# Linear attention and feed-forward on one core: k side of a batch first, k shifted by its maxima in PSUM, and a job order read from a table

## The chip, the cores and the metric

The kernel runs on one core of a Trainium2 chip. The metric is device microseconds of one execution. Each comparison below is made in rounds on one chip, in which the kernel under test and the kernel before run by turns; ratios and their intervals use only executions in the fast state. PE is TensorE, DVE is VectorE, ACT is ScalarE, POOL is GpSimd, SP issues most of the DMA. "Profiled run" is one execution with the trace on.

## The reference, cut to what matters

```python
def phi(x):                                     # q, k: 8 batches x 8 heads x 576 x 64
    proj = einsum('bhsd,df->bhsf', x, w_phi)    # 128 features
    proj = proj - max(abs(proj), axis=-1)
    return concatenate([exp(proj), exp(-proj)], axis=-1)
q_p, k_p = phi(q), phi(k)
kv = einsum('bhsf,bhsd->bhfd', k_p, v);  z = sum(k_p, axis=2)
x  = (q_p @ kv) / (q_p . z + 1e-6)              # then heads side by side: 8 x 576 x 512
xn = layernorm(x) * g_ln
out = x + relu(xn @ w_ch1) @ w_ch2              # 512 -> 2048 -> 512
```

The maximum is subtracted before both exponentials, so `exp(-proj)` becomes `exp(m) * exp(-proj)` and `exp(proj)` becomes `exp(-m) * exp(proj)`, with m the maximum of one token.

## The kernel before

The batches are worked in four pairs. A pair has eight units of attention, and then its tokens go through the feed-forward layer in chunks of token tiles (128 tokens each). While PE does one pair's feed-forward, the other engines do the next pair's attention. The first pair has nothing before it to hide behind. Its inputs are transposed by PE; later pairs use DMA transposes.

Every piece of work is a job that says which engine may do it, how long it is thought to take, and which data it reads and writes. A list scheduler in the kernel, run when the program is built, turns the jobs into one order for each engine:

```python
LAG = {"PE": 0.24, "DVE": 0.20, "ACT": 0.23, "POOL": 0.22, "SP": 0.1, "DMA": 1.8, "CAST": 1.8}
class Order:
    def add(self, alts, rank, emit, r=(), w=(), acquire=None, release=None, lag=None, rows=False, early=0.0): ...
    def due(self): ...    # ranks from a backward pass            # ... cut
    def run(self): ...    # forward simulation, takes the most urgent ready job per engine   # ... cut
...
    with tc.manual_schedule(engines={ET.PE, ET.DVE, ET.Activation, ET.Pool, ET.SP}):
        sched.due()
        sched.run()
```

The k side multiplies v, on POOL, by exp(m) and by its reciprocal, for both signs of the exponential:

```python
        def scale_main(t):                       # L640, for t = 1 and t = 0
            e = (u.get("en"), u["em", 1])[t]     # exp(-m), exp(m)
            nc.gpsimd.tensor_tensor(out=u["vv"][:, t, 0:MX, 0:D],
                in0=vb[:, uu, :].rearrange("p (c d) -> p c d", d=D),
                in1=bcast(e[:, 0:MX], 2, D), op=ALU.mult)
            # ... cut: the column of e, and the tail tokens
        add("DVE", 0.13, V, en, r=[("em", 1, n % 3)], w=[("en", n % 3)])
        for e in range(2):
            add("ACT", 0.96, V, lambda e=e: exps(e), r=[("pm", 1, n, e), ("m", 1, n % 3, e)],
                w=[("EB", e, n % NE)], release=[("B", 1)])
        add("POOL", 1.5, V, lambda: scale_main(1), ...)
        add("POOL", 1.5, V, lambda: scale_main(0), ...)
```

The first pair goes unit by unit (k and q of two heads, all tokens), and asks for the weights after units 2, 3, 5 and 6. Its first feed-forward chunk, three tiles, needs all heads of the first batch, so four units:

```python
    TILES0 = 1;  sizes = (3, 3, 3)
    WEIGHTS = {2: (0, 1), 3: (2, 3), 5: (4, 5), 6: (6, 7)}
```

Of the kernel before, what the change touches and what calls it, by code (L numbers as in the profile page):

```python
# [13 lines left out]
ALU = mybir.AluOpType  # L14
# [9 lines left out]
LAG = {"PE": 0.24, "DVE": 0.20, "ACT": 0.23, "POOL": 0.22, "SP": 0.1, "DMA": 1.8, "CAST": 1.8}  # L24


STAY = 10.0


class Op:  # L30
    __slots__ = (
        "alts", "emit", "rank", "lag", "users", "acquire", "release",
        "ready", "left", "number", "rows", "taken", "at", "early",
    )


class Order:


    def __init__(self, room):  # L40
        self.ops, self.wrote, self.read, self.room = [], {}, {}, dict(room)

    def add(
        self, alts, rank, emit, r=(), w=(), acquire=None, release=None, lag=None, rows=False,
        early=0.0
    ):
        op = Op()
        op.alts, op.emit, op.rank, op.lag = alts, emit, rank, lag
        op.early = early
        op.acquire, op.release, op.rows, op.taken = acquire, release, rows, False  # L50
        op.number, op.users, op.ready, op.at = len(self.ops), [], 0.0, None
        deps = {self.wrote[k].number: self.wrote[k] for k in (*r, *w) if k in self.wrote}
        for k in w:
            deps.update({o.number: o for o in self.read.get(k, ())})
        for o in deps.values():
            o.users.append(op)
        op.left = len(deps)
        for k in w:
            self.wrote[k], self.read[k] = op, []
        for k in r:  # L60
            self.read.setdefault(k, []).append(op)
        self.ops.append(op)
        return op

    def due(self):

        waiting, free, events = {}, {}, []
        before, left, ready = {}, {}, {}
        for op in self.ops:
            left[op.number], ready[op.number] = len(op.users), 0.0  # L70
            for o in op.users:
                before.setdefault(o.number, []).append(op)
            for engine in op.alts:
                waiting.setdefault(engine, [])
                free.setdefault(engine, 0.0)
            if not op.users:
                heapq.heappush(events, (0.0, op.number, op))
        rank, taken = {}, set()
        while events:
            now = events[0][0]  # L80
            while events and events[0][0] <= now + 1e-9:
                op = heapq.heappop(events)[2]
                if op is not None:
                    for engine in op.alts:
                        heapq.heappush(waiting[engine], (-op.rank, -op.number, op))
            for engine, queue in waiting.items():
                if free[engine] > now + 1e-9:
                    continue
                op = None
                while queue and op is None:  # L90
                    op = heapq.heappop(queue)[2]
                    if op.number in taken:
                        op = None
                if op is None:
                    continue
                taken.add(op.number)
                end = now + op.alts[engine]
                free[engine], rank[op.number] = end, -end
                heapq.heappush(events, (end, -1, None))
                for o in before.get(op.number, ()):  # L100
                    lag = max(LAG[e] for e in o.alts) if o.lag is None else o.lag
                    same = len(o.alts) == 1 and engine in o.alts
                    n = o.number
                    ready[n] = max(ready[n], end + (0.1 if same else lag))
                    left[n] -= 1
                    if not left[n]:
                        heapq.heappush(events, (ready[n], n, o))
        for op in self.ops:
            op.rank = rank[op.number] - op.early

    def run(self):
        waiting, free, room, events, done = {}, {}, self.room, [], []
        rows = False

        def offer(op):
            heapq.heappush(events, (op.ready, 1, op.number, op, None))

        for op in self.ops:
            for engine in op.alts:
                waiting.setdefault(engine, [])  # L120
                free.setdefault(engine, 0.0)
            if not op.left:
                offer(op)
        now = 0.0
        while events:
            now = events[0][0]
            while events and events[0][0] <= now + 1e-9:
                _, kind, _, op, _ = heapq.heappop(events)
                if kind == 1:
                    for engine in op.alts:  # L130
                        key = op.ready if engine in ("DMA", "CAST") else op.rank
                        heapq.heappush(waiting[engine], (key, op.number, op))
                elif kind == 0:
                    for name, n in op.release or ():
                        room[name] += n
            for engine, queue in waiting.items():
                if free[engine] > now + 1e-9 or not queue:
                    continue
                passed, held, op = [], set(), None
                if engine == "PE" and rows:  # L140
                    near = sorted(i for i in queue if i[2].rows and not i[2].taken)
                    near = [i for i in near if room[i[2].acquire[0]] >= i[2].acquire[1]]
                    if near and near[0][0] < queue[0][0] + STAY:
                        op = near[0][2]
                while queue and op is None:
                    item = heapq.heappop(queue)
                    op = item[2]
                    if op.taken:
                        op = None
                        continue  # L150
                    if op.acquire is None or (
                        op.acquire[0] not in held and room[op.acquire[0]] >= op.acquire[1]
                    ):
                        break
                    held.add(op.acquire[0])
                    passed.append(item)
                    op = None
                for item in passed:
                    heapq.heappush(queue, item)
                if op is None:  # L160
                    continue
                op.taken, op.at = True, (now, engine)
                if op.acquire:
                    room[op.acquire[0]] -= op.acquire[1]
                us = op.alts[engine]
                if engine == "DMA" and free.get("CAST", 0.0) > now:
                    shared = free["CAST"] - now
                    us = 4.0 * us if 4.0 * us <= shared else us + shared * 0.75
                end = now + us
                if engine == "PE" and op.rows != rows:  # L170
                    rows = op.rows
                    end += 0.1
                lag = LAG[engine] if op.lag is None else op.lag
                free[engine] = end
                done.append((op, engine))
                heapq.heappush(events, (end, 2, op.number, op, None))
                heapq.heappush(events, (end + lag, 0, op.number, op, None))
                for o in op.users:
                    same = len(o.alts) == 1 and engine in o.alts
                    o.ready = max(o.ready, end + (0.1 if same else lag))  # L180
                    o.left -= 1
                    if not o.left:
                        offer(o)
        assert len(done) == len(self.ops)
        for op, engine in done:
            if op.emit:
                op.emit(engine)
        return now
# [3 lines left out]
def kernel(  # L192
# [34 lines left out]
    NKV = 6  # L227
    NXT = 3
    NX = 2
# [9 lines left out]

    wphi_f = consts.tile([P, F], FP32, name="wphi_f")  # L240
    gln_sb = consts.tile([P, KC], FP32, name="gln")
    ident = consts.tile([P, P], BF16, name="ident")
    wbq = consts.tile([P, 2, F], BF16, name="wbq")
    wbk = consts.tile([P, 2, F], BF16, name="wbk")
    eps_sb = consts.tile([P, 1], FP32, name="eps")
# [862 lines left out]
    for n in range(NU):  # L1108
        pair, i = divmod(n, H)
        u = {"pair": pair, "i": i, "n": n, "g": n // HG, "uu": n % HG, "h": i, "slot": i}  # L1110
        if pair == 0:
            u.update(b=i // 4, h=2 * (i % 4))
# [176 lines left out]
```

## Time and profile before

Median 377.4 us; the profiled run's span is 375.2 us.

The page of the kernel before: busy time of each engine with its share of the span, then some of the rows of 40 equal slices (tenths of busy time, tenths of full clock for PEclk).

```profile
PE 349.1 (93%) x3306; PEld 208.0 (55%) x3348; DVE 273.1 (73%) x738; ACT 257.5 (69%) x650; POOL 182.4 (49%) x349
PE   2888789989999899999999999999999999999995
PEclk9998799999999999999999999999999999999998
DMA  6999699999969745493547754712200244010102
```

PE is nearly always busy, except in the first eight or so slices (to about 75 us) and at the very end. That is the stage to look at. Busy times by stretch of the kernel before, in us from the span's start; the columns are the stretch, then PE, PEld, DVE, ACT and POOL busy with counts, the granted clock, the DMA share and GB/s:

```profile
32.00:36.00 4.00, 4.00 (x55) 3.24 (x54) 3.40 (x13) 3.71 (x11) 3.99 (x8) 0.61 1.17 179
44.00:48.00 4.00, 3.93 (x26) 2.01 (x24) 3.37 (x13) 1.05 (x5) 3.58 (x7) 0.50 0.81 178
0.00:40.00 40.00, 27.39 (x324) 18.07 (x324) 30.64 (x91) 30.83 (x80) 28.56 (x63) 0.96 0.97 232
40.00:80.00 40.00, 37.00 (x406) 23.39 (x409) 37.83 (x116) 32.79 (x92) 30.14 (x62) 0.91 1.00 222
80.00:340.00 260.00, 253.99 (x2407) 150.21 (x2443) 199.50 (x526) 186.07 (x466) 123.74 (x226) 1.00 0.53 125
```

In the first 40 us no engine is full: DVE, ACT, POOL and PE share the stage about evenly. The timeline of PE of the same kernel shows the first feed-forward matmuls (hT), at start and duration in us:

```profile
45.51 2.74 PE L1001 MATMUL hT_ps<-xT,w 128*128 128x384 bf16 x8
...
53.32 1.46 PE L1001 MATMUL hT_ps<-xT,w 128*128 128x384 bf16 x8
```

The same eight matmuls take 2.74 us at a clock of 0.50 and 1.46 us at full clock. The two POOL scalings of v, from the table of groups (busy us, mean ns, then idle time before them and what ended it), are these, and each comes with 0.6 to 0.7 us of smaller instructions:

```profile
L645 POOL TENSOR_TENSOR vv<-v,emk 128x512 bf16<-128x512 f32 x32 | 33.5, 1047 | 43.9 <-ACT emk L616 33.3 <-issue 7.9 <-PE ch_ps L1033 1.3
L645 POOL TENSOR_TENSOR vv<-v,en 128x512 bf16<-128x512 f32 x32 | 33.5, 1047 | 0.0
```

**A measure used below.** "Busy" of PE contains latency, and this trace lacks some matmul records (550 of 592 ch records are there), so small idle times cannot be read from it. I therefore also count work: each recorded matmul is given what it costs in a dense stretch, columns / 2.4 plus 2.5 ns. That is the rate the Trainium skill states ("TensorE: Matmul & The Clock Gate", "Wait — 56ns, not 53.3ns?"), and this trace agrees: four hT matmuls of 384 columns take 0.65 us in the chain of waits (formula 0.65), three of 512 take 0.65 (0.647). Matmuls on 64 rows count half (sixteen pm of 128 columns take 0.45 us). By this measure the whole program, without the new shifts, is 320.7 us of PE work with the old jobs and 320.9 with the new ones (one chunk more means 64 more matmuls); I count with 320.8 for all.

### The profile page before, as it was taken

How to read it: one execution, taken by the hardware profiler on the slowest of the kernel's cores; microseconds unless marked ns; L12 is line 12 of the kernel's file. 1: busy time of each engine (PE TensorE's matmuls, PEld its weight loads, DVE VectorE, ACT ScalarE, POOL GpSimd, SP SyncE). 2: the span in 40 equal slices, each digit the busy share in tenths (PEclk: the TensorE clock that was granted, in tenths of full speed). 3: DMA queues.
4: the chain of work that ended last, by engine and by line, in shares of the span. 5: the costliest groups of instructions: out<-in, count | busy, mean ns of one | idle time of the engine just before them, and what ended most of it. 6: DMA issues, size and time to landing. Idle time of an engine off the chain costs nothing.

```text
span 375.2 us, 9069 instructions
## 1 busy us (share of the span) xinstructions
PE 349.1 (93%) x3306; PEld 208.0 (55%) x3348; DVE 273.1 (73%) x738; ACT 257.5 (69%) x650; POOL 182.4 (49%) x349
## 2 busy tenths in 40 slices
PE   2888789989999899999999999999999999999995
PEld 1466456546565555655656555655565546555553
DVE  3889989979879999987879979978788672000102
ACT  3889698799879648876569768966589437433310
POOL 5589989367866434744455537454447320000000
PEclk9998799999999999999999999999999999999998
DMA  6999699999969745493547754712200244010102
GB/s 174 291 281 192 124 223 265 239 233 234 256 145 242 221 114 119 84 237 106 189 141 159 208 130 99 152 39 72 66 2 28 58 114 98 9 48 29 56 30 84
DMA packets 89132, 52.43 MB, mean 140 GB/s; under 512 B 55552, under 2 KB 84608, under 8 KB 89088
## 3 DMA queue, kind: packets, MB, share of 16 engines
q1 hardware_dynamic: 84240, 47.11, 50.9%
q0 software_dynamic: 4224, 4.19, 7.0%
q10 hardware_dynamic: 624, 0.56, 0.5%
q8 instruction: 26, 0.43, 0.5%
q14 instruction: 18, 0.15, 0.1%
HBM read 36.77 MB, written 9.44 MB: 123 GB/s over the span
## 4 chain that ended last, share of the span: by engine, by line
PE 74%; DVE 9%; DMA 6%; ACT 6%; issue 2%; POOL 2%; SPq 0%; DVEq 0%; POOLq 0%
PE ch_ps L1033 30%; PE hT_ps L1001 29%; DMA qkT<-qkb 4%; PE num L738 4%; PE kv L709 4%; PE pm L580 3%; ACT EB L631 3%; DVE m L600 3%; DMA qk<-in_k_dram 2%; ACT ea L684 1%; PE pt L678 1%; DVE numc L744 1%; DVE numc L750 1%; PE kv L704 1%; DVE st L881 1%
## 5 line engine op out<-in xcount | busy, mean ns | idle before, releaser
L1001 PE MATMUL hT_ps<-xT,w 128*128 128x384 bf16 x768 | 150.7, 328 | 1.5 <-DVE m L600 1.0
L1033 PE MATMUL ch_ps<-w,hT 128*128 128x512 bf16 (+2 forms) x550 | 141.0, 373 | 2.7 <-issue 0.9
L1001 PEld LDWEIGHTS <-w 128*128 128x128 bf16 x768 | 71.4, 98 | 54.7 <-issue 5.2
L1011 ACT ACTIVATE hT<-hT_ps 128x384 bf16<-128x384 f32 x119 | 58.5, 496 | 58.9 <-PE hT_ps L1001 58.4
L600 DVE TENSOR_REDUCE m<-pm 128x4 f32<-128x512 f32 x128 | 81.4, 676 | 9.0 <-PE pm L580 8.9
L762 POOL TENSOR_TENSOR x<-numc,rden 128x192 bf16<-128x192 f32 (+1 forms) x112 | 50.4, 461 | 67.4 <-DVE rden L756 65.2
L1033 PEld LDWEIGHTS <-hT 128*128 128x128 bf16 x592 | 53.3, 98 | 47.0 <-issue 2.5
L684 ACT ACTIVATE ea<-pt 128x512 bf16<-128x512 f32 x128 | 69.0, 637 | 7.2 <-PE pt L678 7.1
L631 ACT ACTIVATE EB<-pm 128x512 bf16<-128x512 f32 x128 | 69.0, 634 | 3.0 <-DVE m L600 2.6
L1041 DVE SCALAR_TENSOR_TENSOR o<-ch_ps,rstd,x 128x512 f32<-128x512 f32 (+2 forms) x37 | 26.6, 727 | 54.6 <-PE ch_ps L1033 39.5
L645 POOL TENSOR_TENSOR vv<-v,emk 128x512 bf16<-128x512 f32 x32 | 33.5, 1047 | 43.9 <-ACT emk L616 33.3
L1009 DVE TENSOR_SCALAR hT<-hT_ps 128x384 bf16<-128x384 f32 x73 | 39.0, 542 | 4.9 <-PE hT_ps L1001 4.3
L744 DVE TENSOR_TENSOR numc<-num,emq 128x195 f32<-128x195 f32 (+1 forms) x96 | 32.4, 344 | 10.1 <-PE num L738 8.9
L738 PEld LDWEIGHTS <-ea 128*128 128x128 bf16 x512 | 28.0, 99 | 13.7 <-issue 1.9
L750 DVE TENSOR_TENSOR numc<-numc,num 128x195 f32<-128x195 f32 (+1 forms) x100 | 33.1, 342 | 1.2
L645 POOL TENSOR_TENSOR vv<-v,en 128x512 bf16<-128x512 f32 x32 | 33.5, 1047 | 0.0
L738 PE MATMUL num<-KV,ea 128*128 128x65 bf16 x512 | 31.8, 196 | 1.1 <-ACT ea L684 0.9
L881 DVE BATCH_NORM_STATS2 st<-x 128x6 f32<-128x512 bf16 x36 | 24.4, 677 | 2.1 <-POOL x L762 1.9
L709 PE MATMUL kv<-vv,EB 128*128 128x65 bf16 x512 | 25.0, 199 | 0.0
L580 PEld LDWEIGHTS <-qkT 64*128 64x128 bf16 x512 | 16.8, 99 | 14.2 <-issue 8.2
L890 ACT ACTIVATE xc<-x,mv 128x512 bf16<-128x512 bf16 x19 | 13.8, 725 | 14.6 <-DVE mv L882 12.2
L709 PEld LDWEIGHTS <-EB 128*128 128x128 bf16 x512 | 22.6, 102 | 1.6
(71 smaller groups left out, 371.3 us busy)
## 6 DMA issues: line engine op xcount, KB each, us to landing
out_dram<-o SPq DMA_DIRECT2D x31, 256.0 KB, 2.4
qk<-in_k_dram SPq DMA_DIRECT2D x28, 256.0 KB, 4.6
v<-in_v_dram SPq DMA_DIRECT2D x28, 256.0 KB, 3.7
qk<-in_q_dram SPq DMA_DIRECT2D x26, 256.0 KB, 5.2
w<-in_moe_w_ch_dram POOLq DMA_DIRECT2D x8, 512.0 KB, 9.4
qk<-in_k_dram SPq DMA_DIRECT2D x2, 512.0 KB, 6.8
qk<-in_q_dram SPq DMA_DIRECT2D x2, 512.0 KB, 7.8
v<-in_v_dram SPq DMA_DIRECT2D x2, 512.0 KB, 8.2
```

The costliest lines, as they stand in the source:

```text
L600: nc.vector.reduce_max(out=u["m", i].rearrange("p (c e) -> p e c", e=2)[:, e], in_=u["pm", i, e], axis=AX.X, apply_absolute_value=True,)
L631: nc.scalar.activation(u["EB"][:, t, e * 4 : (e + 1) * 4].rearrange("p c f -> p (c f)"), u["pm", 1, e].rearrange("p c f -> p (c f)"), AF.E ...
L645: nc.gpsimd.tensor_tensor(out=u["vv"][:, t, 0:MX, 0:D], in0=vb[:, uu, :].rearrange("p (c d) -> p c d", d=D), in1=bcast(e[:, 0:MX], 2, D), ...
L684: nc.scalar.activation(u["EA"][:, t, e * 512 : (e + 1) * 512], u["pt", e], AF.Exp, scale=(1.0, -1.0)[t],)
L709: nc.tensor.matmul(ps[:, t, c // 4, :], EB[:, t, (c % 2) * 4 + c // 2, :], vv[:, t, c, :], start=False, stop=(t == 0 and c == MX - 1), ski ...
L738: nc.tensor.matmul(ps[:, t, i, :], lhsT, rhs, start=(j == 0), stop=(j == len(terms) - 1))
L750: nc.vector.tensor_add(out=st["numc"][:, 0:nch], in0=st["numc"][:, 0:nch], in1=st["ps"][:, 0])
L762: nc.gpsimd.tensor_tensor(out=dst, in0=st["numc"][:, i : i + cnt, 0:D], in1=bcast(st["rden"][:, i : i + cnt], 2, D), op=ALU.mult,)
L1001: nc.tensor.matmul(st["ps"][:, 0:cols], w1_sb[:, kc, jj * P : (jj + 1) * P], pr["xT", r][:, kc, 0:cols], start=(kc == 0), stop=(kc == KC - 1),
L1009: nc.vector.tensor_relu(h_sb[:, 0:cols], st["ps"][:, 0:cols])
L1011: nc.scalar.activation(h_sb[:, 0:cols], st["ps"][:, 0:cols], AF.Relu)
L1033: nc.tensor.matmul(ch[t, c0], hT[r, jj][:, rt * P : (rt + 1) * P], w2_sb[:, jj, c0:c1], start=(jj == 0), stop=(jj == JC - 1),)
```

## The change

The intent: let the first feed-forward chunk start sooner, and take POOL's scalings of v out of the first pair's k chain (a small subtraction on POOL, `low_part` below, goes into it). For the first pair only:

- k of all four units of a batch first, then q by token tiles, so that two q jobs complete two tiles; chunks of 2, 2, 2 and 3 tiles.
- v is only cast. PE adds minus m to the projection in PSUM, as two bf16 parts (high part and rest), so that the two exponentials come out scaled.
- Weights are asked for after units 1 to 4.

For the whole program, the scheduler is replaced by a table of all 2558 jobs in order. How it was found is not known.

```diff
-    def due(self): ...
-    def run(self): ...
+    def follow(self, order):
+        for number, engine in order:
+            op = self.ops[number]
+            assert op.before <= done and engine in op.alts, number
+            op.emit(engine) ...
+WORK = """
+0 2 1 10 4 12 8 3 11 6 5 13 14 9 7 16 47 28 48d 15 29 18 49 17 92 50a 93d 19 56 20 51 94 58
+... 2558 entries
+"""
+    def low_part(lo, m):                       # POOL
+        nc.gpsimd.tensor_tensor(out=lo, in0=m, in1=m.bitcast(BF16)[:, 1::2], op=ALU.subtract)
+    def minus_max(ps, m, lo):                  # PE, `minus` is -identity
+        for part in (m.bitcast(BF16)[:, 1::2], lo):
+            nc.tensor.matmul(ps, minus, bcast(part, 2, F), start=False, stop=True, skip_group_check=True)
...
-                        (wbk if i else wbq)[rows, e, :], start=True, stop=True,
+                        (wbk if i else wbq)[rows, e, :], start=(c == 0), stop=True,
...
+            for e in range(2):
+                add("POOL", 0.2, V, lambda e=e: rest(e), ...)
+                add("PE", mm(2, 512), V, lambda e=e: shift(e), ...)
+                add("ACT", 0.96, V, lambda e=e: exps(e), r=[("pm", 1, n, e)], ...)
+            add("POOL", 0.7, V, values, ...)   # cast of v only
...
-    TILES0 = 1
+    TILES0 = 2
-        sizes = (3, 3, 3)
+        sizes = (3, 3, 3) if p_ else (2, 2, 2, 3)
...
-    WEIGHTS = {2: (0, 1), 3: (2, 3), 5: (4, 5), 6: (6, 7)}
+    WEIGHTS = {1: (0, 1), 2: (2, 3), 3: (4, 5), 4: (6, 7)}
...
-        sched.due()
-        sched.run()
+        sched.follow(work(sched.ops))
```

(Cut: the loops that make the jobs, the q jobs, two more buffers, the order of the first loads.) `start=(c == 0)` is needed because only the first matmul into a bank may clear its flags if a later one is to add to all of it: the Trainium skill says that the first matmul of a group clears the whole bank's flags ("PSUM — Partial Sum Buffer", "The four PSUM rules"). The result agrees with the reference. The record marks the runs without shift matmuls as correct too, so that check would not notice a wrong shift.

## The prediction

> **What bounds the kernel now.** The page has PE busy 93% of the 375.2 us span, DVE 73%, ACT 69%, POOL 49%. By stretches, PE is busy 197 of 200 us from 140 to 340 us: PE-bound there, and nearly so from 60 us on. The first stage is not: in 8 to 44 us PE is busy about 29 of 36 us, latency included; at steady rates (four 384-column matmuls in 0.65 us, three of 512 in 0.65, the 18 of kv in 0.75) I estimate only 20 us of PE work there. In 20 to 40 us DVE has 17.6, ACT 18.1, POOL 17.7 of 20. The first feed-forward matmul (hT) runs at 45.5 us. The granted clock is 0.61 in 32-36, 0.74 in 40-44, 0.50 in 44-48 us; the first eight hT take 2.74 us, the next 1.46. That agrees with the Trainium skill, "TensorE: Matmul & The Clock Gate", Part 1 (activity releases the throttle, idling restores it). I estimate 4 us lost to it.
>
> **What the change does to the first pair.**
> - Removes both POOL scalings of v (1.05 + 0.41 + about 0.25 us, twice a unit: 3.4); a copy and small subtractions replace them (about 1.2, from the 1.04 of a 1024-element cast). Some 17 us of POOL over eight units. ACT loses emk (0.24 a unit), DVE en (0.20) and the first weight casts (3.3).
> - Adds on PE 32 matmuls of 512 columns (0.215 each) and 8 of 256: 7.7 us.
> - Reorders: k sides first, then q by token tiles, so tiles 0 and 1 are complete after two q jobs; first chunk of 256 columns; weights asked for earlier.
> - Later pairs keep their work; the order is frozen.
>
> **Critical path.** By the table, before the first hT PE has about six k and four q jobs (estimates 2.4 and 1.7 us: 21 us), DVE and ACT 25 to 27 us. From 8.5 us on that puts the first hT at 36 to 39 us, some 8 earlier. But then about 12 us of first-pair PE work is still to come, against 8 in the old kernel at 45.5 (matmul counts by stretch). Net 3 to 4 us from the order, 3 to 4 from a clock that stays up, as the shifts keep PE active. About six of the 7.7 us of shifts fall into idle PE time. POOL's saving is worth little alone: DVE and ACT still bound the stage. The tail (4 us of idle PE) stays.
>
> **Prediction: 370 us, 8 in 10 between 363.5 and 377.** Faster by over 2%: 0.47; within 2%: 0.46; slower by over 2%: 0.07.
>
> **What would show it.** First hT between 35 and 40 us; PE busy in 20 to 40 us 18 or more, clock there above 0.95; POOL busy down by 15 us or more; PE from 140 to 340 us still 98 to 99%; DVE still the fullest after PE before 45 us.
>
> **What would make it wrong.**
> - DMA: almost full from 20 to 100 us except 28 to 47. The queues' shares are 191 us for 47 MB and 26 for the weights, so first-pair inputs plus weights last until about 53 us. Earlier weights may delay the second batch's k, q, v; PE, in a fixed order, then waits at their transposes or at the weights: 375 or more.
> - The fixed order may suit late DMA transposes badly (10.3 and 4.9 us of them in the chain of waits at 61 to 80 us).
> - The shifts lengthen the chain from maxima to exponentials; with eight PSUM banks this may hold back k jobs.
> - If the 6 us of PE idle between 45 and 140 us vanish as well: 363.

## The result, and the profile after

371.8 us (median, 371.25 to 372.09) against 377.4 (376.82 to 377.68): ratio 0.9852, interval 0.9834 to 0.9869. A ratio is the mean time of one kernel's fast runs over that of the other's in the same rounds, so it is not quite the ratio of the medians quoted. The time lies inside the range of the prediction, 1.8 us above its centre, and the change is 1.5% faster, so within 2%.

The page of the changed kernel, same rows:

```profile
PE 350.9 (95%) x3452; PEld 212.7 (58%) x3452; DVE 262.2 (71%) x728; ACT 261.9 (71%) x661; POOL 168.5 (46%) x333
PE   3976889999999999999999999999999999999995
PEclk9996999999999999999999999999999999999999
DMA  7999999999874562499559776331200233001022
```

The clock still dips, now in the fourth slice, and the DMA engines are full without the earlier gap. The stretches of the changed kernel:

```profile
28.00:32.00 4.00, 1.72 (x21) 0.79 (x18) 3.15 (x9) 3.19 (x8) 3.25 (x10) 0.65 1.18 246
32.00:36.00 4.00, 3.31 (x20) 1.86 (x21) 1.56 (x7) 1.81 (x4) 0.76 (x2) 0.50 1.17 247
0.00:40.00 40.00, 28.16 (x346) 16.99 (x347) 26.70 (x76) 30.18 (x69) 24.64 (x64) 0.91 1.06 241
40.00:80.00 40.00, 37.71 (x489) 27.85 (x488) 38.11 (x127) 37.52 (x110) 25.85 (x51) 1.00 1.10 245
80.00:340.00 260.00, 259.48 (x2472) 154.26 (x2472) 192.90 (x521) 186.77 (x469) 118.04 (x220) 1.00 0.49 121
```

Up to 80 us the two kernels differ little in PE's busy time. After 80 us PE is busy 259.5 of 260 us, with every record there. PE's timeline of the changed kernel says what happened at 30 us and when the first hT ran:

```profile
32.69 0.61 PE L587 MATMUL qkT_ps<-ident,qk 128*128 128x128 bf16 x4 [2.43 <-DMA qk<-in_q_dram]
...
42.18 0.60 PE L1080 MATMUL hT_ps<-xT,w 128*128 128x256 bf16 x4 [0.32 <-ACT EB L669]
```

PE stood 2.43 us waiting for the second batch's first q. The clock had fallen before that: in stretches of 0.5 us it is at half from about 29.2 to 36.0 us, and the wait began at about 30.3. A second trace of the same kernel (the run "again" below, with the same time) was expected to show this stall again. From its list of PE's waits from 8 to 60 us:

```profile
PE qkT_ps L587 <- DMA qk<-in_k_dram: 1.8, 1, 1.8
...
PE qkT_ps L587 <- DMA qk<-in_q_dram: 0.4, 1, 0.4
```

PE lost 1.8 us early to a k load, so it came later to the wait for q, which was 0.4 us; yet the first hT ran at 42.4 us. What the two traces share is not the length of the wait but the time at which q landed, 32.6 and 32.2 us. The DMA issues say why it was late. First the kernel before, then the changed one; the columns are KB written and us from issue to landing, each for that same q load, and the weights' median from the page:

```profile
qk<-in_q_dram SPq DMA_DIRECT2D x1, 512.0 KB, 7.9
w<-in_moe_w_ch_dram POOLq DMA_DIRECT2D x8, 512.0 KB, 9.4
```

```profile
qk<-in_q_dram SPq DMA_DIRECT2D x1, 512.0 KB, 17.1
w<-in_moe_w_ch_dram POOLq DMA_DIRECT2D x8, 512.0 KB, 17.7
```

The q load, issued at 15.5 us, took 17.1 us instead of 7.9 (issued at 13.0). The weight loads went on beside it: POOL issued the first of them at 11.7 us (in the kernel before at 24.8) and all eight before q landed. The Trainium skill says that transfers started by different engines run on the same 16 DMA engines and interleave ("DMA: Bandwidth & Descriptors", "Issuing engines are not separate DMA queues"); the two sets of numbers agree with that.

The shifts in the changed kernel, and the cast that replaces the scalings, from its table of groups:

```profile
L426 PE MATMUL pm<-m,minus 128*128 128x512 bf16 x16 | 7.3, 459 | 0.0
L426 PE MATMUL pm<-lo,minus 128*128 128x512 bf16 x16 | 7.2, 452 | 0.0
...
L711 POOL CAST vb<-v 128x512 bf16<-128x512 f32 x8 | 4.9, 614 | 0.5 <-DMA v<-in_v_dram 0.4
L715 POOL CAST vb<-vx 128x130 bf16<-128x130 f32 x8 | 2.4, 297 | 0.0
```

Each matmul's duration contains latency; in a dense stretch they follow each other every 0.22 us, so all 40 shift matmuls are 7.8 us of work.

Where the 5.3 us between the spans (375.2 and 369.9) come from, by the measure of work:

| | before | after |
|---|---|---|
| PE work done by 80 us, without shifts | 42.6 | 43.7 |
| time from 80 us to the end | 295.2 | 289.9 |
| unfilled time after 80 us | 17.0 | 12.8 |

So the rebuilt first pair has put the kernel 1.1 us ahead at 80 us (0.4 if the three missing records are added), although it also did 7.8 us of shifts by then. The other 4.2 us come after 80 us, where the jobs are nearly the same as before. That was not what I had predicted, and most of the experiments are about it. PE's waits from 80 to 345 us, longest in total first (us in total, times, longest), are these in the kernel before and, in the second fence, in the changed one:

```profile
PE hT_ps L1001 <- DVE m L600: 1.0, 1, 1.0
PE ch_ps L1033 <- issue: 0.9, 6, 0.2
PE xT_ps L947 <- DVE hT L1009: 0.9, 1, 0.9
PE hT_ps L1001 <- ACT EB L631: 0.4, 1, 0.4
...
```

```profile
PE hT_ps L1080 <- DVE numc L823: 0.5, 2, 0.4
```

Of PE's short waits for DVE and ACT, 3.1 us in the whole list before, 0.5 us are left. ("issue" gaps of 0.2 us may be missing records.)

### The profile page after: what moved, and what is told of

It reads as the page before. It is cut to its first block, busy times and chain, and to the rows that moved or that the text cites. A ratio compares the mean times of both kernels' runs of the same rounds, so it can differ in the third digit from the quotient of the medians.

```text
span 369.9 us, 9296 instructions
## 1 busy us (share of the span) xinstructions
PE 350.9 (95%) x3452; PEld 212.7 (58%) x3452; DVE 262.2 (71%) x728; ACT 261.9 (71%) x661; POOL 168.5 (46%) x333
## 4 chain that ended last, share of the span: by engine, by line
PE 79%; DMA 9%; DVE 5%; ACT 5%; issue 1%; POOL 0%; ACTq 0%; DVEq 0%; POOLq 0%
PE ch_ps L1112 32%; PE hT_ps L1080 31%; DMA qk<-in_q_dram 6%; PE num L811 4%; PE pm L611 4%; PE kv L781 3%; ACT EB L669 2%; DMA qkT<-qkb 2%; PE pt L749 2%; ACT ea L755 1%; DMA kx<-in_k_dram 1%; DVE numc L817 1%; PE px L454 1%; DVE numc L823 1%; DVE hT L1088 1%
## 5 line engine op out<-in xcount | busy, mean ns | idle before, releaser
L1112 PE MATMUL ch_ps<-w,hT 128*128 128x512 bf16 (+2 forms) x592 | 147.0, 373 | 0.0
L1080 PE MATMUL hT_ps<-xT,w 128*128 128x384 bf16 (+1 forms) x832 | 142.6, 314 | 1.3 <-DVE numc L823 0.5
L1080 PEld LDWEIGHTS <-w 128*128 128x128 bf16 x832 | 78.6, 98 | 49.2 <-issue 1.4
L1090 ACT ACTIVATE hT<-hT_ps 128x384 bf16<-128x384 f32 (+1 forms) x139 | 65.1, 479 | 48.1 <-PE hT_ps L1080 47.1
L835 POOL TENSOR_TENSOR x<-numc,rden 128x192 bf16<-128x192 f32 (+2 forms) x104 | 49.9, 493 | 56.1 <-DVE rden L829 51.0
L683 POOL TENSOR_TENSOR vv<-v,emk 128x512 bf16<-128x512 f32 x24 | 25.2, 1048 | 39.1 <-ACT emk L653 21.0
L1088 DVE TENSOR_SCALAR hT<-hT_ps 128x384 bf16<-128x384 f32 (+1 forms) x69 | 33.9, 501 | 5.1 <-PE hT_ps L1080 4.7
L823 DVE TENSOR_TENSOR numc<-numc,num 128x195 f32<-128x195 f32 (+1 forms) x100 | 32.7, 340 | 0.7
L811 PE MATMUL num<-KV,ea 128*128 128x65 bf16 x512 | 30.3, 195 | 0.9 <-ACT ea L755 0.8
L683 POOL TENSOR_TENSOR vv<-v,en 128x512 bf16<-128x512 f32 x24 | 25.1, 1046 | 2.4 <-DVE en L676 1.3
L976 POOL TENSOR_TENSOR xc<-mv,x 128x512 bf16<-128x512 f32 x13 | 13.4, 1040 | 12.1 <-DVE mv L961 6.3
## 6 DMA issues: line engine op xcount, KB each, us to landing
w<-in_moe_w_ch_dram POOLq DMA_DIRECT2D x8, 512.0 KB, 17.7
qk<-in_q_dram SPq DMA_DIRECT2D x4, 512.0 KB, 12.5
v<-in_v_dram SPq DMA_DIRECT2D x3, 512.0 KB, 11.7
```

The lines of the kernel that those rows point to most:

```text
L683: nc.gpsimd.tensor_tensor(out=u["vv"][:, t, 0:MX, 0:D], in0=vb[:, uu, :].rearrange("p (c d) -> p c d", d=D), in1=bcast(e[:, 0:MX], 2, D), ...
L811: nc.tensor.matmul(ps[:, t, i, :], lhsT, rhs, start=(j == 0), stop=(j == len(terms) - 1))
L823: nc.vector.tensor_add(out=st["numc"][:, 0:nch], in0=st["numc"][:, 0:nch], in1=st["ps"][:, 0])
L835: nc.gpsimd.tensor_tensor(out=dst, in0=st["numc"][:, i : i + cnt, 0:D], in1=bcast(st["rden"][:, i : i + cnt], 2, D), op=ALU.mult,)
L1080: nc.tensor.matmul(st["ps"][:, 0:cols], w1_sb[:, kc, jj * P : (jj + 1) * P], pr["xT", r][:, kc, 0:cols], start=(kc == 0), stop=(kc == KC - 1),
L1088: nc.vector.tensor_relu(h_sb[:, 0:cols], st["ps"][:, 0:cols])
```

## The experiments

Theory after the result: the gain comes from the table's order of the later pairs; the first stage gained little, because it became bound by what DMA delivers. The rivals: the new jobs give the gain, and the table only records it; or the stage is bound by PE, or by DVE and ACT. All twelve kernels ran in five rounds; the letter in the table names the chip, and runs of one letter share their runs of the kernel before. Medians are of all runs; order_old_sched and shift_only have one slow run each, and their fast runs alone have medians of 380.4 and 376.5.

| run | median us | ratio to before | interval |
|---|---|---|---|
| changed kernel, first measurement | 371.8 | 0.9852 | 0.9834 to 0.9869 |
| changed kernel, again (chip B) | 371.9 | 0.9836 | 0.9809 to 0.9863 |
| order_old_sched (A) | 380.8 | 1.0107 | 1.0072 to 1.0141 |
| double_shift (A) | 372.9 | 0.9904 | 0.9881 to 0.9928 |
| no_shift_mm (A), wrong | 373.3 | 0.9911 | 0.9887 to 0.9934 |
| late_w2 (A) | 372.8 | 0.9895 | 0.9872 to 0.9919 |
| early_q2 (B) | 372.2 | 0.9842 | 0.9816 to 0.9868 |
| late_weights (B) | 369.7 | 0.9783 | 0.9757 to 0.9810 |
| shift_only (B) | 376.6 | 0.9933 | 0.9893 to 0.9974 |
| table_first (C) | 381.7 | 1.0116 | 1.0082 to 1.0151 |
| sched_first (C) | 373.3 | 0.9902 | 0.9872 to 0.9932 |
| late_weights_no_shift (C), wrong | 371.9 | 0.9856 | 0.9828 to 0.9885 |
| late_weights_zero_shift (D), wrong | 370.0 | 0.9821 | 0.9795 to 0.9847 |

### The new jobs under the old scheduler

```diff
-class Order: follow() and the table
+class Order: due() and run() of the kernel before
-        sched.follow(work(sched.ops))
+        sched.due()
+        sched.run()
```

> All jobs of the changed kernel, but put in order by the old kernel's own list scheduler instead of the table. My theory: most of the 5.6 us gained comes from waits of PE that the table takes away after 40 us (PE idle from 40 to 340 us was 8.9 us before and is 2.9 after), so without the table the time is 374 to 379 us and PE idle from 40 to 340 us is 6 us or more. Rival: the new jobs give the gain and the table only records what a scheduler would do: 371 to 373 us.

Measured 380.8 us, 1.1% slower than the kernel before. The rival falls: the new jobs without the table lose. The run is also above my 374 to 379. The scheduler's constants were made for the old jobs, so this is no proof that the new jobs cannot be scheduled by rule.

### Which part of the table

The table was cut after its 617th entry, the last one of the first pair's attention (about 70 us), and one side given to the old scheduler's order:

```diff
-        sched.follow(work(sched.ops))
+        auto = sched.due_and_run()          # the old scheduler's order, as a list
+        head = first 617 entries of the table
+        table_first: head, then auto without the jobs of head
+        sched_first: auto's order of the jobs of head, then the rest of the table
```

> The changed kernel's jobs; the table's order up to the end of the first pair's attention (its first 617 entries, about 70 us), the old list scheduler's order for the rest. The whole under the old scheduler was 380.8 (1.0107 of the kernel before), with the table 371.9 (0.984). My theory: most of that 9 us lies after 70 us, where PE's idle time was 3.5 us from 140 to 340 us under the scheduler and 0.35 with the table; then this run is at 376 to 380. Rival: the table's worth lies in the first stage, where it packs the new jobs: 371 to 374.

> The mirror image: the old scheduler's order for those first 617 entries, the table's order after. My theory: 372 to 376 us. Rival: 378 to 381. Both this and its mirror near 376 would mean that the table's worth is spread over both; both above 380 would mean that the seam itself costs too much to tell.

Measured on chip C: 381.7 us with the table first, 373.3 with the table second. Most of the worth of the table lies in its second part: with the new jobs the ratio is 1.0107 without the table, 1.0116 with its first part alone, 0.9902 with its second part alone and about 0.984 with both. The stretch from 80 to 340 us, of sched_first in the first fence and of table_first in the second:

```profile
80.00:340.00 260.00, 260.00 (x2507) 155.55 (x2504) 193.78 (x529) 190.03 (x479) 120.55 (x222) 1.00 0.48 119
```

```profile
80.00:340.00 260.00, 255.76 (x2458) 151.25 (x2457) 203.79 (x534) 186.23 (x464) 114.73 (x213) 1.00 0.49 121
```

Both have all their matmul records (as many as weight loads, or more by the window's edge), so these idle times are real: none and 4.2 us. Note DVE, too: 203.8 us busy under the scheduler's later order, 193.8 under the table's. A seam could have cost something, but then before 80 us; the measure of work keeps the two apart:

| profiled run | work by 80 us | unfilled after 80 us |
|---|---|---|
| before (old order throughout) | 42.6 | 17.0 |
| table_first (old order after 70 us) | 40.9 | 18.1 |
| sched_first (table after 70 us) | 40.3 | 12.0 |
| after (table throughout) | 43.7 | 12.8 |
| late_weights (table throughout) | 44.9 | 12.5 |

Every kernel listed whose later pairs follow the table leaves 12 to 13 us unfilled (seven more such traces, counted alike, leave 11.2 to 13.5); the two under the old scheduler leave 17 to 18, with different first pairs. About 5 us are thus the later order's. table_first is behind at 80 us as well, which I put down to the seam; no run separates that.

### What the shifts cost

double_shift adds, in each shift, two matmuls of the same size that add zeros. no_shift_mm leaves the shift matmuls out (wrong, which the check against the reference does not notice).

```diff
-        for part in (m.bitcast(BF16)[:, 1::2], lo):
+        for part in (m.bitcast(BF16)[:, 1::2], lo, zero, zero):      # double_shift
+        for part in ():                                              # no_shift_mm
```

> Every shift has two more matmuls of the same size that add zeros, 7.7 us more PE work in the first stage, result unchanged. My theory: part of it falls into PE's idle time before the first hT, so 2 to 5 us slower than the changed kernel (374 to 377). Rival A: PE is the limit all through, the full 7.7 us show (379 to 380). Rival B: the shifts are hidden altogether, under 1 us (372 to 373).

> Wrong on purpose: the shift matmuls are left out, all else stays. My theory: 2 to 4 us faster than the changed kernel (368 to 370), as much as they cost beyond the idle time. If they are hidden: 371 to 372. If they cost their full 7.7 us: 364.

On the same chip A the two took 372.9 and 373.3 us, with ratios of 0.9904 and 0.9911. So 15.6 us of shifts and none at all take the same time. My estimate that some of the shifts' cost would show was wrong: the first stage of the changed kernel is not bound by the amount of PE's work. (The changed kernel itself did not run on chip A; on other chips its ratio was 0.984 to 0.985.) The stretch from 20 to 40 us, of double_shift and then of no_shift_mm:

```profile
20.00:40.00 20.00, 17.90 (x246) 11.29 (x243) 18.56 (x57) 19.14 (x45) 12.99 (x31) 1.00 1.18 238
```

```profile
20.00:40.00 20.00, 11.08 (x154) 7.59 (x148) 14.94 (x49) 15.18 (x35) 11.24 (x25) 0.74 1.18 236
```

The DMA share is the same 1.18. Without the shifts PE comes sooner to the wait for q (4.2 us instead of 2.4) and is at half clock from about 29.8 to 43.1 us; with double the shifts that wait is 0.2 us and the clock never falls. So equal times are a net result: what the run without shifts saves in work it may lose by its clock. The work by 80 us, shifts left out, is 41.6 us without them, 43.7 in the changed kernel and 43.5 with double shifts, so the second 7.8 us of shifts did fall into idle time, by one trace of each.

### When the loads land

> Only the four loads of the second layer's weights are issued later, at about 30 us instead of 19 and 26 us. My theory: they delay the second batch's q, which lands at 32.7 us while PE waits for it 2.4 us and then runs at half clock for some 6 us. With them later q lands by about 28 us, that wait is under 0.5 us, the granted clock in 20 to 40 us is above 0.93 instead of 0.83, the first hT runs at 39 us or sooner, and the time is 367 to 370. Rival: DVE and ACT bound this stage, and the wait only replaces one for them: 371 to 372.5.

```diff
 table, POOL's entries:
-  ... kx1, w2 loads 5 and 4, x q0, lo k4, w2 loads 7 and 6, x q1 ...
+  ... w2 loads 5 and 4 before the last lo k6, w2 loads 7 and 6 before the last lo k7 ...
```

Measured 372.8 us: not faster. This theory fell as stated. In the trace the four loads are issued only at 42.5 and 47.2 us, later than planned. It shows q issued at 18.0 us and landing after 16.1, at 34.1 us, so later than in the changed kernel (32.6): the second layer's weights were not what it waited for. While q was under way, the four loads of the first layer were.

> The second batch's first q load is issued just after its k load, before the k and v tails and v; bytes and all else unchanged. After the last group my theory is that the first stage of the changed kernel is bound by when the one DMA queue of SP delivers, in the order of issue, not by the second layer's weights. Then q lands by 26 us instead of 32.7, the 2.4 us wait and the half clock at 28 to 36 us go, and PE's first hT runs at 40 us or sooner (42.2). Time: 369 to 371.5 if the next loads (k, v, q of the last group, at 37, 41 and 45 us) then hold PE in its place only in part; rival, that the total of the loads bounds the stage whatever their order: 371.5 to 373.

```diff
     load_main(k, 2, [0, 1], "SP", 3.0)
+    load_main(q, 2, [0, 1], "SP", 3.1)
     load_tails(k, 0, [1], "SP", ...)
     load_main(v, 2, [0, 1], "SP", ...)
     load_tails(v, 0, [1], "SP", ...)
-    load_main(q, 2, [0, 1], "SP", 3.4)
```

Measured 372.2 us beside 371.9 of the unaltered kernel on the same chip B. q landed at 23 us (issue at 11.8, 11.1 us to land), but the load now behind it took its place:

```profile
26.35 0.22 PE L444 MATMUL xT_ps<-ident,kx 128*128 128x128 bf16 x1 [2.43 <-DMA kx<-in_k_dram]
```

That is PE's timeline of early_q2: the same 2.43 us, for the k tail. Changing places in the queue did not help, as the rival had it.

> All weight loads but the first two are issued later (second pair at about 26 us instead of 16, the second layer's at about 30 us), so that the queue of k, q and v has the DMA engines more to itself between 13 and 30 us. Theory: q of the second batch lands by 29 us and the last q by 41 us instead of 45.5; the clock in 20 to 40 us is above 0.93; time 367 to 371. If the loads are not what matters: 371.5 to 373. If the weights then come too late for hT at 50 to 60 us: 373 or more.

```diff
 table, POOL's entries:
-  w1 loads 3 and 2 after values k2 (16 us), w2 loads 5 and 4 after kx1 (19 us), 7 and 6 after lo k4 (26 us)
+  w1 loads 2 and 3 before the last lo k5, w2 loads 4 and 5 before the last lo k6, 6 and 7 before the last lo k7
```

Measured 369.7 us, on chip B beside 371.9 for the unaltered kernel: 2.1 us less, and a ratio of 0.9783 to the kernel before. In the trace the moved loads are issued at 30.7, 37.6 and 42.4 us instead of 15.9, 19.1 and 25.7, so 15 to 19 us later, more than planned. The same q load now, from issue at 17.3 us:

```profile
qk<-in_q_dram SPq DMA_DIRECT2D x1, 512.0 KB, 10.6
```

It lands at 27.9 us, the last q at 34.6 instead of 45.5, and PE waits for neither. The clock falls to half at about 29.3 us here too, with no wait for q, but is back by 32.7 instead of 36.0. The first hT in late_weights' timeline of PE, and its stretch from 20 to 40 us:

```profile
39.60 0.60 PE L1076 MATMUL hT_ps<-xT,w 128*128 128x256 bf16 x4 [0.65 <-ACT EB L665]
```

```profile
20.00:40.00 20.00, 16.26 (x218) 10.39 (x215) 18.48 (x61) 19.17 (x47) 12.71 (x29) 0.91 1.14 252
```

DVE and ACT are now 92 to 96% busy there, against 15.7 and 16.6 us before the edit: the stage is handed back to them. The expectation of a clock above 0.93 was just missed (0.91).

### The shifts alone in the old order

The old kernel, its unit order and its scheduler, with only the shift of the diff above put in.

> The old kernel with its job order rule and its list scheduler, and only the k scaling moved from POOL to shifts in PSUM by PE. Theory: POOL's saving alone is worth little, PE gets 7.7 us more work of which most is hidden: 375 to 379 us beside 376.7. Rival, that POOL's chain was what held back the first stage: 370 to 373.

Measured 376.6 us, 0.9933 of the kernel before, with a wide spread (372.9 to 377.0 in fast runs). So the shift as a whole is worth about 0.7% there, in spite of the added PE work: it takes the scalings off POOL, but also emk off ACT and en off DVE, and the weight loads now wait for the last subtraction in place of the last scaling. No run separates these. My theory's range holds, and the rival's does not.

### Do the shifts help by keeping the clock up?

> Wrong on purpose: the variant with later weight loads (369.7 us) without the shift matmuls. Without them the unaltered table got no faster (373.3 against 371.9): PE came sooner to its wait for q and its clock was at half for 12 us. If deliveries and DVE and ACT set the pace of the first stage also with the weights late, this is 368.5 to 371. If the shifts' 7.7 us of PE work were hidden only by the late q, they show now: 363 to 367.5.

> Wrong on purpose: the variant with later weight loads, with shift matmuls of the same number and size that add zeros and wait for no subtraction of POOL. Without any shift matmuls that variant took 371.9 us (0.9856 of the kernel before) against 369.7 (0.9783) with them, and the clock in 20 to 40 us was 0.71 against 0.91. Theory: the shifts' PE work keeps the clock up, so with zero shifts the clock there is 0.88 or more and the ratio 0.976 to 0.981 (369 to 370.5). Rival: the table was fitted to the timing that the shifts' chain gives, or the two groups of runs merely differ: the ratio stays near 0.985 (371 to 373).

```diff
-        for part in (m.bitcast(BF16)[:, 1::2], lo):
+        for part in ():                    # late_weights_no_shift
+        for part in (zero, zero):          # late_weights_zero_shift
```

Without shift matmuls 371.9 us (0.9856), with zero shifts 370.0 (0.9821), with real ones 369.7 (0.9783), each on another chip. The stretch from 20 to 40 us of the run without, then of the one with zeros:

```profile
20.00:40.00 20.00, 15.59 (x204) 11.11 (x199) 18.56 (x61) 19.37 (x48) 12.37 (x28) 0.71 1.19 245
```

```profile
20.00:40.00 20.00, 16.42 (x231) 10.62 (x229) 18.49 (x60) 19.18 (x46) 11.97 (x27) 0.91 1.12 239
```

The clock follows the PE work: 0.71 without, 0.91 with work that computes nothing. It is so in every run: the mean granted clock of a whole execution is 0.975 to 0.986 without shifts, 0.994 to 1.000 with zeros, 0.992 to 0.998 with real ones. The time points the same way, but the ratio of the zero shifts lies between the two ranges that I had set and its interval overlaps that of the run without. So it is shown that the shifts cost no net time here also when q comes in time, and that they hold the clock up. That they gain time by it is not settled. The work by 80 us in these profiled runs (45.2 without shifts, 44.4 with zeros, 44.9 with real ones) does not show it.

## Why the prediction was right or wrong

The time was right: 370 predicted, 371.8 measured, inside the range, and "within 2%" had a chance of 0.46 (faster by over 2% had 0.47). That was luck: the sum that led there was wrong in its terms.

- **"PE-bound there" from 60 us on, and "Later pairs keep their work; the order is frozen".** This is the step that failed: I gave the later pairs no gain, and named the vanishing of PE's idle time from 45 to 140 us only as a way to be too high. By the measure of work, 4.2 of the 5.3 us come after 80 us, and the two hybrids show that it is the table's order there: 12 to 13 us unfilled with it, 17 to 18 with the old scheduler.
- **"Net 3 to 4 us from the order", for the first stage.** Measured 1.1 us at most by 80 us. The first hT ran at 42.2 us, not at 36 to 39. The order of k before q is not enough by itself: under the old scheduler the new jobs were 1.1% slower than the old kernel. With later weights the first hT runs at 39.6 us and the kernel is 2.3 us ahead by 80 us.
- **"3 to 4 from a clock that stays up".** Wrong for the changed kernel: the clock was 0.65 and 0.50 in 28 to 36 us, 0.83 over 20 to 40 us. From the stretches of 4 us, the clock's deficit to 80 us adds up to some 5.1 us before and 3.4 after, so about 1.7 us were regained, and they are part of the 1.1 us net.
- **"Earlier weights may delay the second batch's k, q, v; PE, in a fixed order, then waits at their transposes."** Right in that q came late and PE waited for it, 2.43 us in one trace and 0.4 in another. The half clock cannot be put down to that wait: it began about 1 us before it, and also in late_weights, which has no such wait. I put this risk beside the sum and not into it. Asking for the weights early cost 2.1 us, as late_weights shows. My first version of it (the second layer's loads) was wrong; late_weights differs from late_w2 chiefly in the second pair of the first layer's loads, at 30.7 us instead of 16.0.
- **"About six of the 7.7 us of shifts fall into idle PE time."** The work is right, 7.8 us. None and 15.6 us of shifts take the same time, so no net cost shows; the clock has a part in that.
- **POOL busy down by 15 us or more:** 182.4 to 168.5, so 13.9. **PE busy in 20 to 40 us 18 or more:** 14.6, and 16.6 in the second trace. **DVE fullest after PE:** ACT was the fullest of all (30.2 us in the first 40, PE 28.2, DVE 26.7).
- **The tail stays:** yes.

The terms erred in both directions, and they cancelled: too much for the first stage, nothing for the later ones.

What stays open: why exactly the table's later order leaves PE fewer waits. DVE is busy about 7 to 10 us less after 80 us with it, and from 80 to 340 us the changed kernel gives it 55 of the relu evictions (28.2 us) where the kernel before gave it 66 (35.2 us). The two hybrids split in the same way (sched_first 56, table_first 68); but no run changes that alone.

## What to carry to other kernels

A change that rebuilds one stage and also replaces the order of everything should be measured as two changes: run the new jobs under the old order, and each half of the new order alone, before saying which stage gained. When a stage has spare DMA time and work is moved forward into it, look at which loads are in flight with the ones that are waited for next; here 2 us came back from asking for six of the eight weight loads 15 to 19 us later. The length of one wait is a poor measure of such a delay: it depends on how early the waiting engine arrives. An engine that is busy 98% by the profile can still hide several us of unfilled time, which counting work against time shows.

## What the Trainium skill lacked or had wrong

- "TensorE: Matmul & The Clock Gate", "Why this matters for your kernels", gives the rule of no idle gaps over about 3 us. Here the clock fell to 0.61 at 32 to 36 us and 0.50 at 44 to 48 us in the kernel before, whose longest single wait of PE from 8 to 45 us was 1.1 us. Its section "A second HAM failure mode: psum-queue depth-cycling" does name frequent small gaps as a cause, but with no size: the clock fell at about 31.7 and 41.9 us, and in the 4 us before PE was busy for 2.17 us (27.7 to 31.7) and 2.23 us (38 to 42).
- No page proposes PE work that computes nothing to hold the clock up in the middle of a kernel, in a stage that is bound elsewhere: zero shifts kept it at 0.91 where it was 0.71 without them, at no net cost in time (370.0 us against 371.9, on two chips).
- "DMA: Bandwidth & Descriptors" says that queues interleave, but not what it costs: the same 512 KB load took 7.9 us with no weight loads beside it, 17.1 us when all eight of POOL's weight loads were issued between 4 us before it and its landing, 16.1 us with four of them (late_w2), and 10.6 us with only two. The weight loads themselves went from 9.4 to 17.7 us.
